# One row of 1024 of most weight chunks goes to GpSimd and ScalarE in the way back of both attentions

## The chip, the cores and the metric

The kernel runs on one core of one Trainium2 chip. The metric is the time of one execution in microseconds (us) of device time, as the median of several executions. The engines are named as in the profile: PE is TensorE, PEld its weight loads, DVE is VectorE, ACT is ScalarE, POOL is GpSimd, and SP is SyncE, which here only issues transfers.

## The reference

A decoding step of four layers for one token, forward and backward: attention, MLP, the same attention again, the same MLP again. Both attentions share `wq`, `wo` and the caches, both MLPs share `w1`, `b1` and `w2`. All data are bf16.

```python
x = x + A(layernorm(x)); x = x + B(layernorm(x))
x = x + A(layernorm(x)); x = x + B(layernorm(x))

# A: D = 1024, 32 query heads, 4 key/value heads, Dh = 128, window W = 4096 of 32768 rows
q = (x @ wq).reshape(32, 128)
p = softmax(q @ k[:, -W:].T * Dh ** -0.5)
return (p @ v[:, -W:]).reshape(4096) @ wo

# B: F = 3584
h = x @ w1 + b1
return (h * tanh(softplus(h))) @ w2
```

The outputs are the step's result and the gradients of all eight arguments for a given gradient of the result: 1024 numbers for `x`, the caches' gradients (two tensors of 4 x 32768 x 128, zero outside the window), and `wq`, `wo`, `w1`, `w2`, `b1`. The core writes 98.6 MB to HBM in all.

## The kernel before

Weights come from HBM in chunks of 1 MB into a ring of eight slots. `Ring.want` lists them in the order of use, and `Ring.pump` (L51, transfer at L68) issues the next load on SP's queue as soon as `Ring.release` has freed a slot. A load therefore waits on SP until the engines that read the old chunk are done with it. The ring's order in the part that matters is `wo` of the second attention (kept from the forward pass), the eight chunks of `wq`, seven of `w2`, eight of `wo`, and five of `wq`; three chunks of `wq` (5, 6 and 7) stay in the ring from one attention's way back to the other's.

The gradient outputs' zero parts are 56 transfers of 1 MB from a tile of zeros. `zeros(n, after)` (L240) issues `n` of them on GpSimd's queue, after a tiny copy on GpSimd that waits for the tile `after`. They are put by hand where they fill the transfer engines.

The way back goes through the second MLP, the second attention (`attn_bwd(1, ...)`), the first MLP, and the first attention (`attn_bwd(0, ...)`). At the end, units of outer products make the weights' gradients, which are evicted into staging tiles and stored from SP's queue (L967, L972).

`attn_bwd` (L822) has two passes over weights. The first multiplies all 4096 rows of `wo` (eight chunks with four rows of 1024 to a partition) with the gradient. The second does it with `wq`, whose chunk `t` has 4096 columns, taken as four pieces of 1024. Between them lie the gradients of the softmax. Each "row" (a 128 x 1024 piece) is done in one of two ways:

- `rowdot` (L401, instruction at L408): one VectorE instruction multiplies the row by the broadcast vector in PSUM (`LB[0]`) and sums it up; the products go to `junk`.
- `turned` (L427): TensorE transposes the row in eight blocks into a PSUM tile (L431), `evac` (L278) copies it back over the row on VectorE (L284) or ScalarE (L287), and later `mv` (L441, instruction at L443) multiplies the eight turned blocks by the vector's columns.

`evac` picks the engine by a running account of charged microseconds, `load`, which `even()` levels. `later` (L415) holds the `mv` calls back until more than `behind[0]` of them wait; a chunk's release stands in the same queue behind its last `mv`. Since everything is issued in this order and each engine works its queue in order, a release is as late as the `mv` ahead of it.

With `DENSE = 2` chunks 0 and 1 of each pass have all four rows turned. From chunk 2 on VectorE does row 0 and the others are turned. In the pass over `wq` of `attn_bwd(0)` the three kept chunks are turned already (`turned_q`).

```python
            behind[0] = max(2, 6 - max(0, c - DENSE + 1))
            rows_chunk(ch, c, GA, l, LB[0], do32, DA, 0 if c < DENSE else 1, None)
            later(lambda c=c: ring.release((*wo_key, c)))
            hooks["do"](c)
```

The hooks put other work between the chunks of the second attention's way back: `conv` turns blocks of the caches, `w1_rest` blocks of `w1`, both with eight transposes and an eviction each.

Of the kernel before, what the change touches and what calls it, by code (L numbers as in the profile page):

```python
# [9 lines left out]
FP32 = mybir.dt.float32  # L10
BF16 = mybir.dt.bfloat16
ACT = mybir.ActivationFunctionType
# [3 lines left out]
P = 128  # L16
# [67 lines left out]
def kernel(  # L84
# [36 lines left out]
    def sb(shape, dtype, name):  # L121
        return keep.tile(shape, dtype, name=name)
# [152 lines left out]
    def even():  # L275
        load["D"] = load["A"] = max(load.values())
# [29 lines left out]
    def bcast(col_of, n, dst=None):  # L306


        for i in range(n):
            k = i % 8  # L310
            nc.tensor.transpose(LB[i // 8][:, k * P:(k + 1) * P], col_of(i).to_broadcast([P, P]), ident_bf[:])  # L311
        if dst is not None:
            nc.vector.tensor_copy(dst, LB[0][:, 0:n * P])
# [84 lines left out]
        return gn  # L398


    def rowdot(w, vecs, n, acc, fours=False):  # L401

        for i, vec in enumerate(vecs):
            out, a = junk[:, 0:n], w[:, i * n:(i + 1) * n]
            if fours:
                out, vec = (x.rearrange("a (k p) -> a k p", p=P) for x in (out, vec))
                a = a.rearrange("a (p k) -> a k p", k=4)
            nc.vector.tensor_tensor_reduce(out=out, in0=a, in1=vec, scale=1.0,  # L408
                                           scalar=acc if i else 0.0, op0=ALU.mult, op1=ALU.add, accum_out=acc)
        load["D"] += len(vecs) * (n * 1.1e-3 + 0.18)  # L410

    lag = deque()
    behind = [2]
# [13 lines left out]
    def turned(w, n, mv, eng=None, block=None):  # L427

        b = big().bitcast(BF16)
        for i in range(n):  # L430
            nc.tensor.transpose(b[:, i * P:(i + 1) * P], block(w, i) if block else w[:, i * P:(i + 1) * P], ident_bf[:])  # L431
        evac(w, b[:, 0:n * P], eng, cost=(0.69 * n / 8, n / 8))
        later(mv, True)
# [7 lines left out]
    def mv(w, n, out, rhs_of, last):  # L441
        for i in range(n):
            nc.tensor.matmul(out, lhsT=w[:, i * P:(i + 1) * P], rhs=rhs_of(i), start=fresh[0], stop=last and i == n - 1,  # L443
                             skip_group_check=True)
            fresh[0] = False

    def rows_chunk(ch, c, col, l, vec, dst, off, nr=2, eng="A"):

        for tt in range(4):
            r = 4 * c + tt  # L450
            if tt < nr:
                rowdot(ch[:, tt, :], [vec], D, dst[:, r:r + 1])
            else:
                w = ch[:, tt, :]
                turned(w, TD, lambda w=w, r=r: mv(w, TD, TP[:, off + r:off + r + 1], lambda i: col[:, i, l:l + 1], True), eng)

    def rows_join(dst, n, off):
        v = dst[:, 0:n].rearrange("p (a b) -> p a b", b=4)[:, :, 2:4]
# [131 lines left out]
    def conv(n, eng=None):  # L590
        for _ in range(n):
            conv_ev(conv_pe(1), eng)
# [224 lines left out]
                rowize_f()  # L817
        return ln_bwd(dnp, sB0["n32"], sB0["rstd"], g, "B0")

    DENSE = 2  # L820

    def attn_bwd(l, sv, g, wo_key, wq_key, wq_keep, hooks, beside=None):  # L822
        name = f"A{l}"
        nc.vector.tensor_copy(GA[:, :, l], g[:])
        bcast(lambda c: GA[:, c, l:l + 1], TD)
        do32 = tmp([P, HQ], FP32, "da")
        mv_open()
        even()
        for c in range(8):
            ch = ring.get((*wo_key, c))  # L830

            behind[0] = max(2, 6 - max(0, c - DENSE + 1))
            rows_chunk(ch, c, GA, l, LB[0], do32, DA, 0 if c < DENSE else 1, None)
            later(lambda c=c: ring.release((*wo_key, c)))
            hooks["do"](c)
        flush()
        for x, n0, k0 in ((0, DENSE, 0), (DENSE, 8, 1)):
            nc.vector.tensor_copy(do32[:, 4 * x:4 * n0].rearrange("p (c k) -> p c k", k=4)[:, :, k0:],
                                  TP[:, DA + 4 * x:DA + 4 * n0].rearrange("p (c k) -> p c k", k=4)[:, :, k0:])
        do_n = from_fours(do32[:])  # L840
        dov = DOC[:].rearrange("p v (g u l h) -> p v g u l h", g=G, u=2, l=2)
        do4 = do_n.rearrange("p (g h) -> p g h", g=G)
        nc.vector.tensor_copy(dov[:, 0, :, 0, l, :], do4)
        nc.gpsimd.tensor_copy(dov[:, 1, :, 1, l, :], dov[:, 0, :, 0, l, :])
        pr = small[:, 64:128]
        prv = pr[:].rearrange("p (g u h) -> p g u h", g=G, u=2)
        o4 = sv["o32"][:].rearrange("p (g h) -> p g h", g=G)
        for u in range(2):
            nc.vector.scalar_tensor_tensor(out=prv[:, :, u, :], in0=do4, scalar=float(D), in1=o4, op0=ALU.mult, op1=ALU.mult)
        sdp = small[:, 224:288]  # L850
        pxv = PX[:].rearrange("p (b l h) -> p b l h", l=2, h=8)
        dsv = DSX[:].rearrange("p (b l h) -> p b l h", l=2, h=8)
        for i in range(2):
            for t in range(16 * i, 16 * i + 16):
                for g_ in range(G):
                    c = scol(g_, t) - 512 * i
                    nc.tensor.matmul(SC[i][:, c:c + 8], lhsT=VS[:, g_, t, :],
                                     rhs=DOC[:, 0, g_ * 32 + l * 8:g_ * 32 + l * 8 + 8], start=True, stop=True)
            if i == 0:
                nc.tensor.matmul(TP[:, 320:384], lhsT=onesD[:], rhs=pr[:], start=True, stop=True)  # L860
                nc.vector.tensor_copy(sdp[:], TP[:, 320:384])
            s = SC[i].rearrange("p (tp c) -> p tp c", c=64)
            nc.vector.tensor_tensor(out=s, in0=s, in1=sdp[:, None, :].to_broadcast([P, 8, 64]), op=ALU.subtract)
# [12 lines left out]
        bcast(lambda c: DQC[:, c, l:l + 1], TD)  # L876
        even()
        hooks["dq"]()
        mv_open()
        bigs.append(SC[1])  # L880
        nc.vector.memset(dnp[:, 0:DENSE], 0.0)
        for t in range(TD):
            key = (*wq_key, t)
            ch = ring.get(key)
            nr = 0 if t < DENSE else 1
            behind[0] = max(2, 6 - max(0, t - DENSE + 1))
            if nr:
                rowdot(ch[:, 0:D], LB[0:1], D, dnp[:, t:t + 1])
            for k in range(nr, 4):
                h0 = 8 * k  # L890
                w = ch[:, h0 * P:(h0 + 8) * P]
                f = lambda w=w, h0=h0, t=t, k=k: mv(w, 8, TP[:, t:t + 1], lambda i: DQC[:, h0 + i, l:l + 1], k == 3)
                if key in turned_q:
                    later(f, True)
                else:
                    turned(w, 8, f)
            if t in wq_keep:
# [22 lines left out]
        zeros(4)  # L920

    def dq3():
        w1_rest(2)
        zeros(3, DQC[:, 0, 1:2])

    def dn3(t):
        if t % 2:
            w1_rest(1)
        if t == 5:
            zeros(1, dnp[:, t:t + 1])  # L930

    g2 = attn_bwd(1, sA1, g3, ("o", 1), ("q", 2), KEEP_Q2,
                  dict(do=lambda c: conv(2), dp=dp3, dq=dq3, dn=dn3))


    W1S = W1[:].rearrange("p t f -> p (t f)")
# [197 lines left out]
        load["D"] += 10  # L1134
        work(4)

    g0 = attn_bwd(0, sA0, g1, ("o", 3), ("q", 3), (), dict(do=do1, dp=dp1, dq=dq1, dn=dn1), units_a0)
# [49 lines left out]
```

## Time and profile before

| | |
|---|---|
| median of 3 runs | 461.53 us (460.98 to 462.93) |
| the profiled execution | 462.39 us, of which 460.62 are its span |
| PE, PEld, DVE, ACT, POOL busy | 337.2, 275.3, 261.3, 228.2, 38.6 us |
| moved by DMA | 183.59 MB, mean 399 GB/s |
| L431 transposes into BIG (PE) | 872, 252 ns each |
| L287 evictions of 128x1024 from BIG to the ring (ACT) | 73, 1013 ns each |
| L284 the same on DVE | 36, 691 ns each |
| L408 rows of 1024 from the ring (DVE) | 38, 1216 ns each |

The span starts with the first instruction; what lies around it is 1.77 us. A slice of the page is a fortieth of the span, 11.5 us. Times of one instruction run from its start to its end, and neighbours on an engine overlap a little, so the pitch of a row of them is shorter: 0.92 us for ACT's eviction of 1.01.

### The profile page before, as it was taken

Reading aid. Unit: us, or ns where it says so; the run is one execution under the profiler, and the core shown is the slowest. Engines: PE = TensorE matmul, PEld = TensorE weight load, DVE = VectorE, ACT = ScalarE, POOL = GpSimd, SP = SyncE. Lnnn points to the kernel's source line nnn. Section 1 sums busy time; section 2 is a strip of 40 time slices with the busy share of each in tenths; the row PEclk is TensorE's granted clock in tenths of the full one; section 3 lists DMA queues with packets and bytes.
Section 4 is the critical chain, followed back from the end, with each engine's and each line's share of the span. In section 5 each row is a group of like instructions: output and inputs, shape, how many; then the busy total and the mean of one; then the engine's idle time right before and its main releaser. Section 6 shows DMA issues by size and latency. Waiting matters only on the chain. (4 is left out here: it accounts for less than half of the span.)

```text
span 460.6 us, 14273 instructions
## 1 busy us (share of the span) xinstructions
PE 337.2 (73%) x6385; PEld 275.3 (60%) x6385; DVE 261.3 (57%) x517; ACT 228.2 (50%) x263; POOL 38.6 (8%) x85
## 2 busy tenths in 40 slices
PE   4836435597678788599879898897896876677950
PEld 3736435497668787599779898787791121112530
DVE  6505731383150149678428786475485987878860
ACT  2502001064035369378128573283267988778850
POOL 4000000000111320100210101102111000000000
PEclk9955555555555569799559855597595555555555
DMA  8999999999999999999999999979999999999995
GB/s 340 420 419 419 419 420 416 422 388 392 393 422 424 418 414 414 406 384 386 376 424 334 407 387 371 414 264 408 424 420 421 419 425 421 427 424 419 408 407 227
DMA packets 28379, 183.59 MB, mean 399 GB/s; under 512 B 3706, under 2 KB 3734, under 8 KB 9494
## 3 DMA queue, kind: packets, MB, share of 16 engines
q1 hardware_dynamic: 20162, 123.94, 67.0%
q0 software_dynamic: 8064, 58.72, 30.7%
q8 instruction: 50, 0.82, 0.7%
q14 instruction: 11, 0.09, 0.0%
q10 hardware_dynamic: 92, 0.02, 0.0%
HBM read 83.94 MB, written 98.62 MB: 396 GB/s over the span
## 5 line engine op out<-in xcount | busy, mean ns | idle before, releaser
L287 ACT COPY ring<-BIG 128x1024 bf16<-128x1024 bf16 x73 | 72.2, 1013 | 40.4 <-PE BIG L431 37.7
L431 PE MATMUL BIG<-ident_bf,ring 128*128 128x128 bf16 x872 | 80.0, 252 | 3.8 <-DMA ring<-in_A_wo_dram 2.0
L431 PEld LDWEIGHTS <-ring 128*128 128x128 bf16 x952 | 69.8, 114 | 5.2 <-DMA ring<-in_A_wo_dram 2.3
L995 PE MATMUL wide<-W 2*128 2x512 bf16 x228 | 48.5, 601 | 19.0 <-DVE ring L284 3.6
L408 DVE CUSTOM_DVE_ANT_0 junk<-ring,SC 128x1024 bf16<-128x1024 bf16 x38 | 46.2, 1216 | 4.5 <-DMA ring<-in_A_wo_dram 1.7
L995 PEld LDWEIGHTS <-W 2*128 2x128 bf16 x240 | 10.9, 103 | 54.5 <-issue 53.8
L443 PEld LDWEIGHTS <-ring 128*128 128x128 bf16 x1024 | 38.2, 100 | 4.6 <-ACT ring L287 4.4
L287 ACT COPY KT<-BIG 128x1024 bf16<-128x1024 bf16 x22 | 21.8, 1015 | 32.3 <-PE BIG L582 30.9
L287 ACT CAST ring<-wide 128x1024 bf16<-128x1024 f32 (+1 forms) x38 | 35.2, 998 | 4.9 <-PE wide L995 4.0
L284 DVE COPY ring<-BIG 128x1024 bf16<-128x1024 bf16 x36 | 24.8, 691 | 20.3 <-PE BIG L431 13.1
L284 DVE CAST ring<-wide 128x1024 bf16<-128x1024 f32 (+1 forms) x26 | 30.2, 1200 | 5.7 <-PE wide L995 5.2
L248 POOL DMA_DIRECT2D out_dram<-zt x56 | 29.6, 534 | 6.3 <-DMA out_dram<-zt 5.6
L553 PE MATMUL MV<-OC,ring 128*128 128x1 bf16 x512 | 16.6, 166 | 15.2 <-DMA ring<-in_A_wo_dram 12.6
L287 ACT COPY W<-BIG 128x1024 bf16<-128x1024 bf16 x20 | 18.9, 1151 | 15.7 <-PE BIG L766 15.7
L553 PEld LDWEIGHTS <-ring 128*128 128x128 bf16 x512 | 16.0, 106 | 16.0 <-DMA ring<-in_A_wo_dram 13.2
L284 DVE CAST VS<-wide 128x1024 bf16<-128x1024 f32 (+1 forms) x18 | 21.0, 1190 | 4.1 <-PE wide L995 3.1
L473 PE MATMUL MV<-NA,ring 128*128 128x1 bf16 x512 | 15.0, 165 | 10.9 <-DMA ring<-in_A_wq_dram 10.0
L601 PE MATMUL MV<-NB,W 128*128 128x1 bf16 x448 | 16.2, 172 | 9.2 <-DMA W<-in_B_w_dram 6.5
L408 DVE CUSTOM_DVE_ANT_0 junk<-ring,DSX 128x1024 bf16<-128x1024 bf16 x18 | 22.0, 1224 | 0.6
L601 PEld LDWEIGHTS <-W 128*128 128x128 bf16 x448 | 15.9, 118 | 9.8 <-DMA W<-in_B_w_dram 7.2
L1046 PE MATMUL wide<-W 32*128 32x256 bf16 x128 | 20.4, 403 | 1.4 <-ACT W L287 0.8
L473 PEld LDWEIGHTS <-ring 128*128 128x128 bf16 x512 | 14.3, 103 | 11.6 <-DMA ring<-in_A_wq_dram 10.6
(256 smaller groups left out, 539.1 us busy)
## 6 DMA issues: line engine op xcount, KB each, us to landing
out_dram<-zt POOLq DMA_DIRECT2D x56, 1024.0 KB, 12.7
ring<-in_A_wq_dram SPq DMA_DIRECT2D x27, 1024.0 KB
ring<-in_A_wo_dram SPq DMA_DIRECT2D x24, 1024.0 KB
ring<-in_B_w_dram SPq DMA_DIRECT2D x14, 1024.0 KB
out_dram<-ring SPq DMA_DIRECT2D x9, 1024.0 KB
W<-in_B_w_dram SPq DMA_DIRECT2D x8, 896.0 KB
ring<-in_A_k_cache_dram SPq DMA_DIRECT2D x4, 1024.0 KB
VS<-in_A_v_cache_dram SPq DMA_DIRECT2D x4, 1024.0 KB
```

What stands on the lines that cost most here:

```text
L248: nc.gpsimd.dma_start(dst, zt[:])
L284: nc.vector.tensor_copy(dst, src)
L287: nc.scalar.copy(dst, src)
L408: nc.vector.tensor_tensor_reduce(out=out, in0=a, in1=vec, scale=1.0, scalar=acc if i else 0.0, op0=ALU.mult, op1=ALU.add, accum_out=acc)
L431: nc.tensor.transpose(b[:, i * P:(i + 1) * P], block(w, i) if block else w[:, i * P:(i + 1) * P], ident_bf[:])
L443: nc.tensor.matmul(out, lhsT=w[:, i * P:(i + 1) * P], rhs=rhs_of(i), start=fresh[0], stop=last and i == n - 1, skip_group_check=True)
L473: nc.tensor.matmul(q_ps[:, h:h + 1], lhsT=ch[:, h * P:(h + 1) * P], rhs=NA[:, t, l:l + 1], start=(t == 0 and h == 0), stop=(t == TD - 1), ...
L553: nc.tensor.matmul(y_ps[:, dd:dd + 1], lhsT=ch[:, tt, dd * P:(dd + 1) * P], rhs=OC[:, h, l:l + 1], start=(h == 0 and dd == 0), stop=(h == ...
L601: nc.tensor.matmul(h_ps[:, fb:fb + 1], lhsT=f_block(W1[:, t], fb), rhs=NB[:, t, l:l + 1], start=(t == 0 and fb == 0), stop=(t == TD - 1), ...
L995: nc.tensor.matmul(b[:, 512 * i:512 * i + 512], lhsT=R[at:at + 2, lo:lo + P], rhs=R[at:at + 2, ro + 512 * i:ro + 512 * i + 512], start=Tru ...
L1046: nc.tensor.matmul(b[:, k * 256:(k + 1) * 256], lhsT=RT[32 * g:32 * g + 32, a, tp, :], rhs=YS[32 * g:32 * g + 32, :], start=True, stop=Tru ...
```

## The change

In both passes of both attentions, row 1 of the first chunks (seven of `wo`, five of `wq`) is no longer turned. A new `pool_dot` gives it to GpSimd, which multiplies its two halves of 512 with a copy of the vector in SBUF, and writes fp32 products into scratch. ScalarE then sums each half with an accumulating copy in place, into `pacc`. These sums are queued in `sums`, and `tick()` issues one after each later turned row of the loop. VectorE adds the two halves at the end of the pass over `wo`, and after chunk 6 of the pass over `wq`.

[...]

In the second attention (`l == 1`) the `DENSE` chunks are none: VectorE does row 0 from chunk 0 on. There the products need `junk` as scratch, so `rowdot` writes its own over the row (`over`), and GpSimd's first half of a `wq` row lands where row 0 was. In the first attention two chunks keep row 0 on TensorE, and the scratch lies in `W1`'s space.

The other work is shifted: four of the `conv` units stand ahead of the pass over `wo` and none at chunks 6 and 7, and six `w1_rest` units stand ahead of the pass over `wq` and none inside it. `behind` counts its steps from chunk 1 as before. The order of transfers on SP's queue is the same.

```diff
+    def pool_dot(w, vec, parts, acc):
+        for i in range(2):
+            n = D // 2
+            a, b, out = w[:, i * n:(i + 1) * n], vec[i], parts[i]
...
+            nc.gpsimd.tensor_tensor(out=out, in0=a, in1=b, op=ALU.mult)
+            def add_up(i=i):
+                nc.scalar.activation(parts[i], parts[i], ACT.Copy, accum_out=acc[i])
+                load["A"] += 0.6
+            sums.append(add_up)
+    def tick():
+        if sums:
+            sums.popleft()()
...
             if tt < nr:
-                rowdot(ch[:, tt, :], [vec], D, dst[:, r:r + 1])
+                rowdot(ch[:, tt, :], [vec], D, dst[:, r:r + 1], over=over)
+            elif tt == 1 and pool is not None:
+                pool(ch[:, tt, :])
             else:
...
+                if tt > 1:
+                    tick()
...
         bcast(lambda c: GA[:, c, l:l + 1], TD)
+        nc.scalar.copy(vec_o, LB[0][:, 0:D])
...
+        hooks["first"]()
         for c in range(8):
...
-            rows_chunk(ch, c, GA, l, LB[0], do32, DA, 0 if c < DENSE else 1, None)
+            if c < np_o:
+                node = lambda w, c=c: pool_dot(w, halves(vec_o), parts_o(None), [pacc[:, i, c:c + 1] for i in range(2)])
+            rows_chunk(ch, c, GA, l, LB[0], do32, DA, 0 if c < DENSE else 1, None, node, l == 1)
...
+        nc.vector.tensor_tensor(out=dov4[:, 0:np_o, 1], in0=pacc[:, 0, 0:np_o], in1=pacc[:, 1, 0:np_o], op=ALU.add)
...
-        bcast(lambda c: DQC[:, c, l:l + 1], TD)
+        bcast(lambda c: DQC[:, c, l:l + 1], 2 * TD)
+        nc.scalar.copy(vec_q, ...)
...
             if nr:
-                rowdot(ch[:, 0:D], LB[0:1], D, dnp[:, t:t + 1])
+                rowdot(ch[:, 0:D], LB[0:1], D, dnp[:, t:t + 1], over=l == 1 and t < np_q)
             for k in range(nr, 4):
+                if k == 1 and t < np_q:
...
+                    pool_dot(ch[:, D:2 * D], v, parts_q(ch), [pacc[:, i, t:t + 1] for i in range(2)])
+                    continue
...
+                if k > 1:
+                    tick()
+            if t == np_q + 1:
+                for i in range(2):
+                    nc.vector.tensor_tensor(out=dnp[:, 0:np_q], in0=dnp[:, 0:np_q], in1=pacc[:, i, 0:np_q], op=ALU.add)
...
     def dq3():
-        w1_rest(2)
+        w1_rest(6)
...
     def dn3(t):
-        if t % 2:
-            w1_rest(1)
...
+    nodes3 = ((DSX[:, 0:1024], lambda ch: [small[:, 0:512], DSX[:, 1024:2048].bitcast(FP32)], 7),
+              (DSX[:].rearrange("p (b l h) -> p b l h", l=2, h=8)[:, :, 0, :],
+               lambda ch: [ch[:, 0:1024].bitcast(FP32), small[:, 0:512]], 5))
     g2 = attn_bwd(1, sA1, g3, ("o", 1), ("q", 2), KEEP_Q2,
-                  dict(do=lambda c: conv(2), dp=dp3, dq=dq3, dn=dn3))
+                  dict(first=lambda: conv(4), do=lambda c: conv(2) if c < 6 else None, dp=dp3, dq=dq3, dn=dn3),
+                  (0, 0), nodes3)
...
+    g0 = attn_bwd(0, sA0, g1, ("o", 3), ("q", 3), (), dict(first=lambda: None, do=do1, dp=dp1, dq=dq1, dn=dn1),
+                  (2, 2), ((NV[0], lambda ch: parts1, 7), (NV[1], lambda ch: parts1, 5)), units_a0)
```

More of the change, by code (lines that the diff above doesn't have):

```diff
@@ L398, in ln_bwd, with rowdot @@
         return gn
-    def rowdot(w, vecs, n, acc, fours=False):
+    def rowdot(w, vecs, n, acc, fours=False, over=False):
         for i, vec in enumerate(vecs):
-            out, a = junk[:, 0:n], w[:, i * n:(i + 1) * n]
+            a = w[:, i * n:(i + 1) * n]
+            out = a if over else junk[:, 0:n]
             if fours:
@@ L410, in rowdot @@
         load["D"] += len(vecs) * (n * 1.1e-3 + 0.18)
+    sums = deque()
+    def pool_dot(w, vec, parts, acc):
+        for i in range(2):
+            n = D // 2
+            a, b, out = w[:, i * n:(i + 1) * n], vec[i], parts[i]
+            if len(b.shape) == 3:
+                a, out = (x.rearrange("p (b h) -> p b h", h=b.shape[2]) for x in (a, out))
+            nc.gpsimd.tensor_tensor(out=out, in0=a, in1=b, op=ALU.mult)
[6 more added lines that the diff above has]
+            sums.popleft()()
     lag = deque()
@@ L445, in mv, with rows_chunk @@
             fresh[0] = False
-    def rows_chunk(ch, c, col, l, vec, dst, off, nr=2, eng="A"):
+    def rows_chunk(ch, c, col, l, vec, dst, off, nr=2, eng="A", pool=None, over=False):
         for tt in range(4):
@@ L818, in dn_b0, with halves, attn_bwd @@
         return ln_bwd(dnp, sB0["n32"], sB0["rstd"], g, "B0")
-    DENSE = 2
-    def attn_bwd(l, sv, g, wo_key, wq_key, wq_keep, hooks, beside=None):
+    pacc = sb([P, 2, TD], FP32, "pacc")
+    def halves(ap):
+        return [ap[:, 0:512], ap[:, 512:1024]]
+    def attn_bwd(l, sv, g, wo_key, wq_key, wq_keep, hooks, dense, nodes, beside=None):
         name = f"A{l}"
+        DENSE, DENSE_Q = dense
+        (vec_o, parts_o, np_o), (vec_q, parts_q, np_q) = nodes
         nc.vector.tensor_copy(GA[:, :, l], g[:])
         bcast(lambda c: GA[:, c, l:l + 1], TD)
+        nc.scalar.copy(vec_o, LB[0][:, 0:D])
         do32 = tmp([P, HQ], FP32, "da")
@@ L828, in attn_bwd @@
         even()
+        hooks["first"]()
         for c in range(8):
             ch = ring.get((*wo_key, c))
-            behind[0] = max(2, 6 - max(0, c - DENSE + 1))
-            rows_chunk(ch, c, GA, l, LB[0], do32, DA, 0 if c < DENSE else 1, None)
+            behind[0] = max(2, 6 - max(0, c - 1))
+            node = None
+            if c < np_o:
+                node = lambda w, c=c: pool_dot(w, halves(vec_o), parts_o(None), [pacc[:, i, c:c + 1] for i in range(2)])
+            rows_chunk(ch, c, GA, l, LB[0], do32, DA, 0 if c < DENSE else 1, None, node, l == 1)
             later(lambda c=c: ring.release((*wo_key, c)))
@@ L836, in attn_bwd @@
         flush()
-        for x, n0, k0 in ((0, DENSE, 0), (DENSE, 8, 1)):
-            nc.vector.tensor_copy(do32[:, 4 * x:4 * n0].rearrange("p (c k) -> p c k", k=4)[:, :, k0:],
-                                  TP[:, DA + 4 * x:DA + 4 * n0].rearrange("p (c k) -> p c k", k=4)[:, :, k0:])
+        while sums:
+            tick()
+        dov4 = do32[:].rearrange("p (c k) -> p c k", k=4)
+        tp4 = TP[:, DA:DA + HQ].rearrange("p (c k) -> p c k", k=4)
+        if DENSE:
+            nc.vector.tensor_copy(dov4[:, 0:DENSE, 0:1], tp4[:, 0:DENSE, 0:1])
+        nc.vector.tensor_tensor(out=dov4[:, 0:np_o, 1], in0=pacc[:, 0, 0:np_o], in1=pacc[:, 1, 0:np_o], op=ALU.add)
+        nc.vector.tensor_copy(dov4[:, np_o:, 1], tp4[:, np_o:, 1])
+        nc.vector.tensor_copy(dov4[:, :, 2:], tp4[:, :, 2:])
         do_n = from_fours(do32[:])
@@ L875, in attn_bwd @@
         nc.vector.tensor_scalar(out=DQC[:, :, l], in0=dq_ps, scalar1=scale, scalar2=None, op0=ALU.mult)
-        bcast(lambda c: DQC[:, c, l:l + 1], TD)
+        bcast(lambda c: DQC[:, c, l:l + 1], 2 * TD)
+        nc.scalar.copy(vec_q, LB[1][:, 0:D].rearrange("p (b h) -> p b h", h=8) if len(vec_q.shape) == 3 else LB[1][:, 0:D])
         even()
@@ L880, in attn_bwd @@
         bigs.append(SC[1])
-        nc.vector.memset(dnp[:, 0:DENSE], 0.0)
+        if DENSE_Q:
+            nc.vector.memset(dnp[:, 0:DENSE_Q], 0.0)
         for t in range(TD):
@@ L884, in attn_bwd @@
             ch = ring.get(key)
-            nr = 0 if t < DENSE else 1
-            behind[0] = max(2, 6 - max(0, t - DENSE + 1))
+            nr = 0 if t < DENSE_Q else 1
+            behind[0] = max(2, 6 - max(0, t - 1))
             if nr:
-                rowdot(ch[:, 0:D], LB[0:1], D, dnp[:, t:t + 1])
+                rowdot(ch[:, 0:D], LB[0:1], D, dnp[:, t:t + 1], over=l == 1 and t < np_q)
             for k in range(nr, 4):
                 h0 = 8 * k
+                if k == 1 and t < np_q:
+                    v = vec_q
+                    v = [v[:, 0:64], v[:, 64:128]] if len(v.shape) == 3 else halves(v)
+                    pool_dot(ch[:, D:2 * D], v, parts_q(ch), [pacc[:, i, t:t + 1] for i in range(2)])
+                    continue
                 w = ch[:, h0 * P:(h0 + 8) * P]
@@ L896, in attn_bwd @@
                     turned(w, 8, f)
+                if k > 1:
+                    tick()
+            if t == np_q + 1:
+                assert not sums
+                for i in range(2):
+                    nc.vector.tensor_tensor(out=dnp[:, 0:np_q], in0=dnp[:, 0:np_q], in1=pacc[:, i, 0:np_q], op=ALU.add)
             if t in wq_keep:
@@ L1135, in units_a0 @@
         work(4)
-    g0 = attn_bwd(0, sA0, g1, ("o", 3), ("q", 3), (), dict(do=do1, dp=dp1, dq=dq1, dn=dn1), units_a0)
+    NV = [RT[:, a, 8 * i:8 * i + 8, :].rearrange("p t s -> p (t s)") for a in range(2) for i in range(2)]
+    parts1 = [x.bitcast(FP32) for x in NV[2:]]
+    g0 = attn_bwd(0, sA0, g1, ("o", 3), ("q", 3), (), dict(first=lambda: None, do=do1, dp=dp1, dq=dq1, dn=dn1),
+                  (2, 2), ((NV[0], lambda ch: parts1, 7), (NV[1], lambda ch: parts1, 5)), units_a0)
     g0b = sb([P, TD], BF16, "g0b")
```

## The prediction

> **What bounds the kernel now.** I read the page's slices first, then two-microsecond windows of the way back, then the waits of SP's queue, then the timelines of the engines. Names: *do1* and *dn1* are the `wo` and `wq` passes of `attn_bwd(1)` (192.3-220.1 and 231.7-258.1 us), *do0* and *dn0* those of `attn_bwd(0)` (292.9-317.7 and 329.2-346.6 us).
>
> ```profile
> DMA  8999999999999999999999999979999999999995
> GB/s 340 420 419 419 419 420 416 422 388 392 393 422 424 418 414 414 406 384 386 376 424 334 407 387 371 414 264 408 424 420 421 419 425 421 427 424 419 408 407 227
> ```
>
> The transfers bound the whole: 183.59 MB at the 420 GB/s of an undisturbed slice are 437 us of the 460.6. After 345 us every slice but the last moves 407-426 GB/s, the last eviction (L284, 444.05 + 1.22 us) is over 15 us before the end, and the zeros and stores are a fixed number of bytes. So the chain view, which follows only the last 130 us through compute, misleads here: only time in which the queues run empty or thin can be won, and that lies between 192 and 316 us.
>
> ```profile
> 244.00:246.00 2.00, 2.00 (x57) 2.00 (x54) 1.95 (x5) 1.79 (x2) 0.00 (x0) 1.00 0.72 168
> 246.00:248.00 2.00, 2.00 (x55) 2.00 (x53) 1.62 (x4) 1.93 (x2) 0.00 (x0) 1.00 0.86 336
> 300.00:302.00 2.00, 2.00 (x57) 2.00 (x55) 1.67 (x3) 1.76 (x3) 0.00 (x0) 1.00 0.12 47
> 302.00:304.00 2.00, 2.00 (x56) 2.00 (x55) 1.69 (x4) 1.79 (x3) 0.00 (x0) 1.00 0.76 197
> ```
>
> Columns: PE, PEld, DVE, ACT, POOL, clock, DMA share, GB/s. Two holes, both with PE full. Their cause is in SP's waits: a ring slot is loaded again only when TensorE has finished the chunk in it.
>
> ```profile
> SPq L68 <- PE TP L443: 67.3, 33, 5.3
> ```
>
> ```profile
> 202.05 18.44 SPq L68 DMA_DIRECT2D ring<-in_A_wq_dram  x8
> 244.28 25.42 SPq L68 DMA_DIRECT2D ring<-in_B_w_dram  x7
> 301.38 4.45 SPq L68 DMA_DIRECT2D ring<-in_A_wo_dram  x3
> ```
>
> The holes stand right before the first reload of dn1 (244.28) and of do0 (301.38): the zeros issued before them have run out. Against 420 GB/s the windows lose 3.1 us in 192-226, 2.7 in 244-256, 2.2 in 268-290 and 4.8 in 298-316, some 13 us: the most this change could win. Since the queue is empty at 300 us, what happened to transfers earlier no longer counts there. **The end moves as the first reload of do0 (301.38) moves**, plus what the thin stretch behind it gains.
>
> **The costs of one item**, from these rows (durations) and their pitch back to back:
>
> ```profile
> 300.98 1.21 DVE L408 CUSTOM_DVE_ANT_0 junk<-ring,SC 128x1024 bf16<-128x1024 bf16 x1
> 301.01 1.93 ACT L287 COPY ring<-BIG 128x1024 bf16<-128x1024 bf16 x2 [0.24 <-PE BIG L431]
> 302.51 0.69 DVE L284 COPY ring<-BIG 128x1024 bf16<-128x1024 bf16 x1 [0.31 <-PE BIG L431]
> 301.21 0.61 PE L431 MATMUL BIG<-ident_bf,ring 128*128 128x128 bf16 x8
> 301.66 0.34 PE L443 MATMUL TP<-GA,ring 128*128 128x1 bf16 x8
> ```
>
> A row on VectorE: 1.27 us (with its 0.08 accumulator read). A row over TensorE: 0.45 + 0.20 us of PE at full clock (0.85 + 0.20 at half), and an eviction of 0.92 on ACT or 0.65 on DVE. New are two operations. A *product* is GpSimd's 512-element multiply. Nothing in the trace multiplies there; nearest are
>
> ```profile
> 1.01 0.29 POOL masks.py:199 TENSOR_SCALAR_AFFINE_SELECT ident_bf<-ident_bf 128x128 bf16<-128x128 bf16 x1
> 1.75 3.56 POOL L173 MEMSET zt<- 128x4096 bf16 x1
> ```
>
> 512 elements are 0.45 us at the memset's rate (no input) and 1.16 at four selects (one input). A product reads two tensors, so I take **1.1**, near the select, and carry up to 1.65 (half as much again for the second input). A *sum* is ScalarE's 512 fp32 values with an accumulator: three 128x512 casts at 348.75 us take 0.49 each; I take **0.6** (accumulator read included; DVE's takes 0.08) and carry 0.49 to 0.92, ACT's price of 1024. A row moved to GpSimd so takes 0.65 us from PE and one eviction from ACT or DVE, and gives ACT 1.2 us: for ACT and DVE together it is no saving. It helps only where PE is the bound.
>
> [...]
>
> **do1, worked along the queues.** Before, PE carried 26 rows and 14 conversions of 0.45 us: 16.9 + 6.3 = 23.2 us, plus what half clock (to 196.2) and the broadcast add: 192.3 to 220.1. After: 17 rows, 17.4 us. Now ACT is the bound: copy of the vector 1.0, 14 evictions 12.9, 14 sums 8.4 = 22.3 us from 193.4, so 215.7, some waits at the start, last products at 217.1; DVE has 8 rows and 17 evictions, 21.2 us. Minus 3.0 us, plus one more small operation (0.2): **-2.8**. GpSimd needs 2.2 us a chunk where ACT and DVE need 2.7: hidden, and POOL has no zeros queued in this pass. With sums at 0.85 ACT has 3.5 us more. The first reload is later: a chunk now has two products to queue instead of four, so `behind` frees chunk 0 only in chunk 3, behind 17 evictions where 13 stood, with sums between them; I get 205.3 for 202.05. The four zeros end at 204, so a new hole of some 3 us opens here; the reloads then come bunched (205, 206, 208, ...) and the last of them two us earlier. This hole is paid back by the hole at 244, which closes.
>
> **dn1.** The broadcast is 8 transposes longer (0.85 at half clock) and four `w1_rest` units are moved ahead of the pass: about 3.4 us at half clock, less what the earlier full clock gives; chunk 0 starts at 238.7 for 236.9. After that PE has 19 rows, 12.4 us, in place of 26 rows and 4 units. But GpSimd's first output lands in the chunk's row 0, so it waits for VectorE's row 0, which stands behind four `w1` evictions: first product at 240.8. Five pairs at 2.2 are 11, to 251.8; a last sum 0.6; behind it in ACT's queue stand six evictions, 5.5; last products 0.5: 258.4 for 258.1. **+0.3**; I add 0.6 for clock, below: **+0.9**. Each 0.1 us on a product is 1 us here. Queued behind the waiting sums on ACT are evictions, and behind those PE's buffers; on POOL one zero. Chunk 0 is free some 0.4 us earlier counted from the pass's start.
>
> **w2 and `dn_b0`** (260-292): unchanged; 14 VectorE rows of 1.27 hold them. They shift.
>
> **do0.** Chunk 0 is released after 8 queued rows in place of 9: the walk gives 300.5 for 301.4, chunks 1 and 2 302.0 and 302.9 for 303.57 and 305.51 (**-0.9**). The three `wo` loads they start then run close together, and the thin stretch to 314 gains some **0.5** of its 2 us. GpSimd's pair of chunk 2 is done at 302, in time.
>
> **dn0**: GpSimd ends around 344.4 with two zeros issued in between, its last sum and VectorE's last row at 346.3: no change against 346.6, and zeros cover the queues to 362.
>
> Sum: -2.8 + 0.9 - 0.9 - 0.5 = **-3.3 us**. The profiled execution took 462.39 (span 460.62 + 1.77), which would become 459.1; it lies 0.86 above the median, so the median 461.53 becomes **458.2**.
>
> **Rivals.**
> *GpSimd sets the pace (slower).* At 2.0 us a product dn1 ends at 240.8 + 20 + 6.6 = 267.4 (+9.3), do1 at some 223.5 (+3.4), first reload of do0 unchanged: about +12, 474. The point from which it decides: dn1 costs 10 us for each us that a product takes over 1.07, do1 14 us for each over 1.35 (a pair then exceeds its 2.7 us a chunk), and the other terms give 3.6; so 1.4 us is even and 1.5 is 0.5% slower, 464. For it: two inputs; against it: the select's 1.16 holds four fixed costs. Chance 0.20.
> *Dear sums.* At 0.85 do1 is 0.7 longer instead of 2.8 shorter and dn1 2.3 longer than forecast, ACT's 0.92 + 1.7 a chunk then exceeding GpSimd's pair: +2.5, 464. Against it: the casts' 0.49. Chance 0.08.
> *The new hole costs.* If the queue is not empty before do0, the 3 us at 204 are not paid back by the closed holes and the gain is about 1: 460.5. For it: both come from the same bytes. Chance 0.11.
> *PE loses its clock.* In 312-316, where PE transposes some 40% of the time, the granted clock falls to 0.5; in 308-312, at some 53%, it holds. dn1's two rows in 2.2 us are 40%. [...] At 1.05 us a row PE keeps GpSimd's pace but not the last chunks: +0.6, which I booked; with half clock through do1 too another 1.5, 459.7. Chance 0.06.
>
> **Numbers.** My forecast has 0.55. A measurement of this kernel tells about 0.5%, 2.3 us, from no change, so 459.2 to 463.8 is the same. The forecast's own spread (products 0.9 to 1.2, sums 0.5 to 0.65) is 455 to 460, of which 0.48 is faster and 0.07 the same. GpSimd's pace gives 0.18 to slower and 0.02 to the same, dear sums half of their 0.08 to each, the new hole and the clock all their 0.17 to the same: faster 0.48, same 0.30, slower 0.22. The range goes from 455.0, the forecast's cheap end, to 465.0, where a product takes some 1.53 us; beyond that lies most of GpSimd's rival, and little else.
>
> **What would show it.** Right: the first `wq` reload at 205, a thin window at 204-207; do1's end at 217; no hole at 244 and under 1 us of one before do0; products at 1.1 and sums at 0.6. Wrong: products over 1.45 with ACT waiting for POOL through dn1; a clock of 0.5 in do1; the stretch from do0's first reload to the end longer than 159 us.

## The result, and the profile after

The changed kernel took 466.68 us (median of 4 runs, 464.65 to 467.58) beside 461.25 us for the kernel before (460.91 to 462.93): a ratio of 1.0104, 95% interval 1.0062 to 1.0146. It is slower by 5.4 us, where 3.3 us of gain were forecast. Its profiled execution took 467.58 us with a span of 465.72, 5.1 longer than the span before. Each time is the median of the runs in the fast state; one run of experiment 7, at 474.20 us, was in the slow one.

The slices of the page after (DMA busy in tenths, GB/s moved; a slice is now 11.6 us):

```profile
DMA  8999999999999999989999999879997999999997
GB/s 336 423 418 420 418 419 417 421 398 354 400 421 423 420 420 417 416 335 422 398 423 386 384 375 348 325 257 409 422 425 291 410 412 419 417 420 418 404 407 316
```

The weak slice around 244 us (334 before) has 386 now: that hole closed, as forecast. But the slice around 309 us, thin already, fell to 257 of 264, the one before it to 325 of 414, and slice 31, around 355 us, from 421 to 291. Windows show these places close up, with columns as in the prediction. The kernel before:

```profile
306.00:308.00 2.00, 1.85 (x51) 1.73 (x49) 1.69 (x4) 1.74 (x3) 0.00 (x0) 1.00 0.91 340
350.00:352.00 2.00, 1.24 (x9) 0.32 (x9) 0.00 (x0) 1.30 (x5) 0.00 (x0) 0.50 0.99 414
352.00:354.00 2.00, 1.16 (x9) 0.18 (x6) 1.54 (x2) 2.00 (x3) 0.00 (x0) 0.50 1.03 430
```

The kernel after:

```profile
300.00:302.00 2.00, 2.00 (x61) 2.00 (x59) 2.00 (x4) 0.00 (x0) 0.02 (x1) 1.00 0.17 68
302.00:304.00 2.00, 0.11 (x5) 0.04 (x2) 1.47 (x3) 0.72 (x2) 2.00 (x2) 1.00 0.56 197
306.00:308.00 2.00, 2.00 (x34) 2.00 (x34) 1.06 (x2) 2.00 (x5) 1.87 (x3) 0.53 0.04 8
```

```profile
350.00:352.00 2.00, 2.00 (x39) 1.80 (x37) 0.14 (x1) 2.00 (x6) 1.87 (x3) 0.50 0.25 102
352.00:354.00 2.00, 0.35 (x14) 0.26 (x10) 1.97 (x4) 1.85 (x5) 1.98 (x5) 0.50 0.27 94
```

In 300-302 ScalarE and GpSimd do nothing (0.00 and 0.02 of 2 us), and right behind that TensorE does nothing (0.11). The queues are nearly dry at 300 to 304, as they were before (47 and 197 GB/s); new are the hole at 306 and the one at 350 to 354. What stopped GpSimd stands in its timeline (start, duration, group, and in brackets the idle time ahead of it with what ended it):

```profile
301.98 11.50 POOL L424 TENSOR_TENSOR W<-ring,W 128x512 f32<-128x512 bf16 x10 [4.03 <-DMA W<-W]
...
343.36 9.09 POOL L424 TENSOR_TENSOR W<-ring,W 128x512 f32<-128x512 bf16 x8 [9.11 <-DMA W<-W]
352.39 0.17 POOL L243 COPY pz<-dnp 1x1 f32<-1x1 f32 x1
352.51 1.12 POOL L248 DMA_DIRECT2D out_dram<-zt  x2
```

Two waits for a transfer, `W<-W`: 4.03 us in do0 ahead of chunk 1's product, and 9.11 us in dn0 ahead of chunk 0's. SP's timeline shows which transfers these are, and what they did to the reloads:

```profile
298.88 1.37 SPq L1021 DMA_DIRECT2D W<-W  x2
301.34 7.56 SPq L68 DMA_DIRECT2D ring<-in_A_wo_dram  x3
310.28 10.98 SPq L68 DMA_DIRECT2D ring<-in_A_wq_dram  x5
335.02 1.74 SPq L1021 DMA_DIRECT2D W<-W  x2
```

L1021 is `rowize`, which lays a gradient out as rows for the outer products at the end: that of `GA` at 298.88, that of `DQC` at 335.02. Both write columns of `W1`'s tile below 5120 and read columns below 6656. The change put the first attention's vector and products into the same tile, in `RT`, columns 6656 to 10752. No byte is shared, but the built program has GpSimd's product wait for these transfers. The waits pass down the queues. ScalarE's next instruction is the sum of that product:

```profile
303.17 0.63 ACT L427 ACTIVATE W<-W 128x512 f32<-128x512 f32 x1 [4.32 <-POOL W L424]
```

Behind the sum stand evictions, behind those TensorE's buffers (it sits idle for 3.83 us, to 305.94, until an eviction of ScalarE's has ended), and behind TensorE the release of chunk 1: the three reloads come at 301.3, 307.1 and 308.4, for 301.4, 303.6 and 305.5 before. In dn0 the wait also holds back the zeros: those for `t == 3` stand on GpSimd's queue behind eight products and are issued at 352.5. The queues have run dry by 350.

The bytes moved say what the two waits cost. Against 420 GB/s the queues lose 4.5 us in 304-318 for 1.6 before, and 3.6 in 344-366 for nothing before; behind 430 us, where they run out of work, they lose 2.1 less (3.7 for 5.8). That makes 4.4 of the 5.1 us by which the span grew.

### The profile page after: what moved, and what is told of

It is laid out like the page before. It is cut to its first block, busy times and chain, and to the rows that moved or that the text cites. A ratio compares the mean times of both kernels' runs of the same rounds, so it can differ in the third digit from the quotient of the medians.

```text
span 465.7 us, 13569 instructions
## 1 busy us (share of the span) xinstructions
PE 329.2 (71%) x5953; PEld 266.0 (57%) x5953; DVE 263.4 (57%) x528; ACT 238.6 (51%) x338; POOL 92.8 (20%) x133
## 5 line engine op out<-in xcount | busy, mean ns | idle before, releaser
L454 PE MATMUL BIG<-ident_bf,ring 128*128 128x128 bf16 x672 | 69.0, 271 | 18.4 <-ACT ring L287 16.0
L454 PEld LDWEIGHTS <-ring 128*128 128x128 bf16 x728 | 59.8, 123 | 19.9 <-issue 18.1
L287 ACT COPY ring<-BIG 128x1024 bf16<-128x1024 bf16 x54 | 53.9, 1006 | 21.7 <-PE BIG L454 20.6
L410 DVE CUSTOM_DVE_ANT_0 junk<-ring,SC 128x1024 bf16<-128x1024 bf16 x29 | 35.3, 1216 | 6.4 <-ACT junk L427 2.7
L466 PEld LDWEIGHTS <-ring 128*128 128x128 bf16 x800 | 32.0, 105 | 9.9 <-ACT ring L287 9.3
L284 DVE COPY ring<-BIG 128x1024 bf16<-128x1024 bf16 x30 | 20.4, 689 | 25.3 <-PE BIG L454 19.9
L424 POOL TENSOR_TENSOR W<-ring,W 128x512 f32<-128x512 bf16 x24 | 27.0, 1151 | 14.9 <-DMA W<-W 13.1
L581 PEld LDWEIGHTS <-ring 128*128 128x128 bf16 x512 | 16.0, 106 | 14.3 <-DMA ring<-in_A_wo_dram 13.0
L427 ACT ACTIVATE W<-W 128x512 f32<-128x512 f32 x24 | 15.1, 629 | 15.0 <-POOL W L424 14.9
L287 ACT COPY W<-BIG 128x1024 bf16<-128x1024 bf16 x19 | 17.9, 1169 | 9.0 <-PE BIG L794 9.0
```

The source lines that it names most:

```text
L284: nc.vector.tensor_copy(dst, src)
L287: nc.scalar.copy(dst, src)
L424: nc.gpsimd.tensor_tensor(out=out, in0=a, in1=b, op=ALU.mult)
L427: nc.scalar.activation(parts[i], parts[i], ACT.Copy, accum_out=acc[i])
L581: nc.tensor.matmul(y_ps[:, dd:dd + 1], lhsT=ch[:, tt, dd * P:(dd + 1) * P], rhs=OC[:, h, l:l + 1], start=(h == 0 and dd == 0), stop=(h == ...
```

## The experiments

Two measures are used beside the time: the first reload of do0, and the stretch from it to the end of the span. That stretch is 159.2 us before and 164.4 after, so the loss that shows lies behind 301 us. The first reload comes at the same time in both (301.38 and 301.34). A profile is one execution, though, and executions differ in unchanged code as well: the fourteen profiles reach do1 at 187.7 to 191.9 us, the kernel before at 191.9 and the kernel after at 190.0.

The theories. *W*: the loss comes from the scratch's place, through the two waits for row stores. *C*: it comes from TensorE's clock, which dn1 lost as the fourth rival feared. *P*: products and sums cost time wherever they stand. Each time below is compared with runs of the kernel before on the same chip (medians 460.95 to 461.29 us). The changed kernel has four runs that spread over 2.9 us, so a difference from its median is good to some 1.5 us, by an estimate from that spread.

**1. Only the second attention.**

```diff
-                  (2, 2), ((NV[0], lambda ch: parts1, 7), (NV[1], lambda ch: parts1, 5)), units_a0)
+                  (2, 2), ((NV[0], lambda ch: parts1, 0), (NV[1], lambda ch: parts1, 0)), units_a0)
```

> attn_bwd(1) as in the changed kernel, attn_bwd(0) as before. Theory W (the loss lies in the first attention, where GpSimd waits for row stores into another part of the W1 tile): the second attention's part is nearly neutral, 461 to 462.5 us, with the first reload of do0 at 301 to 303 and no window under 200 GB/s in 346-360. Theory C (the loss comes from TensorE's half clock in dn1 and its longer pass): 464 to 466. Theory P (each product and sum costs wherever it stands): half of the loss, 464.

461.98 us, ratio 1.0004 (0.9977 to 1.0030). First reload of do0 at 301.2, stretch 159.4 us. The second attention's part is neutral, which speaks for W and against C and P. It is also no gain.

**2. Only the first attention.**

```diff
-                  (0, 0), nodes3)
+                  (2, 2), nodes3)      # nodes3 with 0 and 0 rows, conv and w1_rest placed as before
```

> attn_bwd(0) as in the changed kernel, attn_bwd(1) as before. Theory W: all of the loss is here, 465 to 467 us, GpSimd's product of do0's chunk 1 waiting some 4 us and that of dn0's chunk 0 some 9 us for W1's own transfers, and the queues nearly dry for some 4 us around 350. Theory C: dn1 is as before, so 460 to 462. Theory P: 464.

464.83 us, ratio 1.0068 (1.0044 to 1.0091). GpSimd waits 12.0 us for `W<-W`, the second and third reload of do0 come 6.8 and 8.1 us behind the first, and the stretch is 163.6 us. The loss is here, though not all of it: 3.5 us of 5.4, with the second attention nearly free by itself. The two parts do not quite add up. By this time alone P, which expects 464, is as near as W; experiments 1 and 3 part the two.

**3. The first attention's scratch out of the `W1` tile.**

```diff
-            a, b, out = w[:, i * n:(i + 1) * n], vec[i], parts[i]
+            a, b = w[:, i * n:(i + 1) * n], vec[i]
+            out = parts[i] if parts else a          # in place, bf16
...
-                  (2, 2), ((NV[0], lambda ch: parts1, 7), (NV[1], lambda ch: parts1, 5)), units_a0)
+                  (2, 2), ((junk[:], lambda ch: None, 7), (junk[:], lambda ch: None, 5)), units_a0)
```

> The changed kernel with attn_bwd(0)'s vector in the free scratch row (VectorE writes its products over the weight row that it has read) and GpSimd's products written in place over their weight row in bf16: nothing of the first attention's products stands in the W1 tile. Theory W: the waits of 4 and 9 us are gone, dn0 ends 8 us earlier, the queues do not run dry around 350: 461 to 462.5 us, 4 to 5 less than the changed kernel. Theories C and P: products and sums are as many as before, so 465.5 to 467.

460.05 us, ratio 0.9964 (0.9938 to 0.9989): 6.6 us less than the changed kernel, more than W expected. The same places of its windows and of SP's timeline:

```profile
300.00:302.00 2.00, 1.68 (x48) 1.61 (x45) 2.00 (x4) 2.00 (x5) 2.00 (x3) 1.00 0.72 184
302.00:304.00 2.00, 0.78 (x16) 0.69 (x15) 1.92 (x4) 2.00 (x6) 2.00 (x3) 1.00 1.16 410
...
350.00:352.00 2.00, 1.89 (x11) 0.46 (x8) 1.93 (x3) 2.00 (x4) 0.00 (x0) 0.50 1.01 423
```

```profile
299.37 2.71 SPq L68 DMA_DIRECT2D ring<-in_A_wo_dram  x3
```

ScalarE and GpSimd are busy throughout 300-302, the three reloads come within 2.7 us instead of 7.6, and 350-352 moves 423 GB/s instead of 102. As many products and sums are made as in the changed kernel, so P falls. In dn1 the granted clock is 0.50 in 244-252 in both kernels, so the 6.6 us are not C's either.

**4. TensorE kept busy in dn1.**

```diff
+    def spin(n):
+        for i in range(n):
+            nc.tensor.transpose(idle[:].bitcast(BF16)[:, i * P:(i + 1) * P], ident_bf[:], ident_bf[:])
...
+                if l == 1:
+                    spin(4)
                 if key in turned_q:
```

> The changed kernel with four extra TensorE transposes of the identity ahead of each row that TensorE turns in dn1 (into a PSUM bank that nothing reads), so that TensorE stays busy between GpSimd's pairs. Theory C: the granted clock stays at 1.0 from 241 us on, dn1 takes 29 us for 31.0, and the end comes 2 us earlier or more: 462 to 464.5. Theory W: the clock comes back but the end stays within 1 us, 465.5 to 467, as the first reload of do0 is covered by the later waits.

469.42 us, ratio 1.0156 (1.0120 to 1.0192): slower than the changed kernel. Windows of dn1, first of the changed kernel, then of this one:

```profile
236.00:240.00 4.00, 1.85 (x34) 1.73 (x31) 4.00 (x8) 2.26 (x4) 2.43 (x3) 1.00 0.99 416
...
244.00:248.00 4.00, 3.60 (x56) 3.31 (x55) 1.77 (x3) 4.00 (x10) 4.00 (x5) 0.50 1.00 373
```

```profile
244.00:248.00 4.00, 3.04 (x70) 2.75 (x67) 3.14 (x6) 3.77 (x9) 4.00 (x5) 1.00 1.01 399
```

The clock did come back (1.00 for 0.50), but dn1 takes 30.8 us for 31.0, where C expects 29. From the first product to the last sum's read both take 12.1 us (237.57 to 249.66 and 239.54 to 251.63), since GpSimd's ten products, 1.11 us apart, set that time; from there to dn1's end this kernel takes 9.8 us for 10.3, with the extra transposes in it. C falls by its own expectation and by experiment 3. But the kernel is slower than W expects too (465.5 to 467), and where its 2.7 us go is not shown: its profiled execution loses 1.0 us in do1 and 0.9 in `dn_b0`, neither of which the edit touches.

**5 and 6. One pass of the first attention mended at a time.** In 5 only do0 has the edit of experiment 3, in 6 only dn0.

> Of attn_bwd(0)'s two passes only do0 has its vector and products out of the W1 tile; dn0 keeps them there. By the windows the changed kernel loses 3.4 us more than the kernel with both mended in 304-318 (the late reloads of do0) and 3.5 us more in 346-360 (dry queues behind dn0's wait). If the two add up: 463.3 us, reloads of do0 within 1 us of each other from 300 on, and dn0's first product still waiting some 9 us. If dn0's wait alone matters: 466; if do0's alone: 460.

461.70 us, ratio 1.0003 (0.9986 to 1.0021). Reloads at 299.1, 300.8 and 301.7; the wait in dn0 is still there (8.86 us).

> The mirror: only dn0 mended, do0 with its scratch in the W1 tile. If the two add up: 463.2 us, the second reload of do0 still some 5 us behind the first, no thin window in 346-360. If dn0's wait alone matters: 460; if do0's alone: 466.

464.81 us, ratio 1.0090 (1.0065 to 1.0114). The wait in do0 stays (3.90 us; reloads at 299.8, 305.4 and 306.7), and in 348-354 all windows move 422 GB/s or more.

By the medians do0's wait is worth 5.0 us taken away alone (466.68 to 461.70) and 4.8 taken away last (464.81 to 460.05), dn0's 1.9 and 1.7, and both together 6.6. So they nearly add up, but not in the shares that the two expectations rested on (3.4 and 3.5 us by the windows): both missed by 1.6 us. The shares are uncertain. The interval of experiment 6 overlaps that of the changed kernel, and the stretches behind the first reload (164.4 us in the changed kernel, 161.2 in 5, 161.7 in 6, 158.5 in 3) give 3.2 and 2.7. Why the 9 us wait costs no more than the 4 us one can be read from the windows: in do0 the queues are empty already (68 GB/s in 300-302), in dn0 four zeros issued at 332 cover part of it (422 GB/s in 333-345), and the end gives some of the rest back. Behind 430 us the queues lose 3.5 to 3.7 us in the kernels with dn0's wait (the changed one, 2 and 5) and 5.5 to 5.8 in those without it (before, 3 and 6).

**7. The row stores moved behind the products.** The scratch stays in `W1`.

```diff
-        if c == 0:
+        if c == 7:
             rowize(GA, TD, 32, 0)
...
-        rowize(DQC, HQ, 0, NOFF)
         zeros(4, DQC[:, 0, 0:1])
...
-        if t == 4:
-            twins()
         if t == 5:
+            rowize(DQC, HQ, 0, NOFF)
+            twins()
```

> The changed kernel with scratch, products and sums where they are (fp32, in the W1 tile), but the row stores that GpSimd waits for moved behind the last product of each pass: those of GA from chunk 0 to chunk 7 of do0, those of DQC and the twins to chunk 5 of dn0. Theory W (it is the order of these transfers and not the form of the products): 460 to 462 us, no wait of POOL for a transfer of W1, reloads of do0 within 1 us of each other, no thin window in 346-360. Rival F (the in-place bf16 form is cheaper by itself, and that is what gained): 465 to 467. In between if the twins' later start costs at the end.

467.16 us, ratio 1.0139 (1.0108 to 1.0169): as slow as the changed kernel, far from W's number and next to F's. F has no cost to show, though: a product takes 1.15 us and a sum of 512 takes 0.63 in both forms (last section). GpSimd's two waits did go (one of 2.15 us, for an earlier pair of `W<-W` transfers, stands ahead of do0's first product), and the reloads came at 299.4, 302.0 and 302.9. But who else reads the rows now waits for them. The tile `W`'s instructions sat idle for `W<-W` 13.1 us in 2 waits in the changed kernel; here, by cause (us, times),

```profile
  DMA W<-W: 23.3, 7
```

and TensorE's outer products wait as well:

```profile
354.76 0.60 PE L1059 MATMUL BIG<-W 2*128 2x512 bf16 x2 [6.83 <-DMA W<-W]
```

The units that make the stores start later (their first product into `wide` at 358.7 us, 347.5 in experiment 3), and 358-360 moves 48 GB/s. The rows are wanted early, so it is the scratch that has to give way, not the transfers. This run removes W's waits without a gain in time; that W explains the loss rests on experiments 2, 3, 5 and 6.

**8. One sum a row, all products in place.** In both attentions the products stand in their row, and one sum of 1024 takes the place of two of 512.

```diff
-            def add_up(i=i):
-                nc.scalar.activation(parts[i], parts[i], ACT.Copy, accum_out=acc[i])
-                load["A"] += 0.6
-            sums.append(add_up)
+        def add_up():
+            nc.scalar.activation(w, w, ACT.Copy, accum_out=acc[0])
+            load["A"] += 1.1
+        sums.append(add_up)
```

> All products in place in bf16 in both attentions, and ScalarE adds up a row in one instruction of 1024 instead of two of 512. Theory S (the term of my sum that was short is the sum's price, 0.63 + 0.19 us instead of 0.6, and ScalarE holds do1 and dn1): a row costs ScalarE 0.92 + 0.19 = 1.1 us instead of 1.64, do1 is 1 to 3 us shorter and dn1 2 us: 457 to 459 us. Rival (GpSimd's two products of 1.15 us hold the pair, and the hole at 204 takes what do1 gains): 459.5 to 460.5, as with both mended.

458.98 us, ratio 0.9948 (0.9929 to 0.9966). dn1 takes 27.1 us. Which of the two edits did that, experiment 10 tells.

**9. Experiment 8 without the second attention.**

> The kernel with one sum a row (458.98 us), but attn_bwd(1) as before: only the first attention has GpSimd's rows. If the second attention's part carries its share now that its sums are cheap (its dn1 took 27.1 us there for 28.4 before, and do0's first reload came at 298.5 for 301.4): 461 us, 2 more than with both. If what happens before the queues run empty at 300 does not count and do0 alone gains: 459.

460.17 us, ratio 0.9989 (0.9963 to 1.0015). The interval, 459.5 to 461.9 us, holds the first expectation and no change, and not the second: the second attention carries a share, some 1.2 us by the medians. The first reload of do0 does not show it: it comes at 298.4 here and at 298.5 in experiment 8, since the pass over `w2` ends at 280.7 us in both (more on this at 12).

**10. All products in place, two sums a row.**

```diff
-    nodes3 = ((DSX[:, 0:1024], lambda ch: [small[:, 0:512], DSX[:, 1024:2048].bitcast(FP32)], 7),
+    nodes3 = ((DSX[:, 0:1024], lambda ch: None, 7),
               (DSX[:].rearrange("p (b l h) -> p b l h", l=2, h=8)[:, :, 0, :],
-               lambda ch: [ch[:, 0:1024].bitcast(FP32), small[:, 0:512]], 5))
+               lambda ch: None, 5))
```

> All products in place as in the kernel with one sum a row, but two sums of 512 a row again. It parts that kernel's 1.1 us over the kernel with only the first attention's products in place. If the sums' price is what counts there (0.55 us of ScalarE a row): 460 us, dn1 29.5 us. If it was the scratch of the second attention (the 3 us that its first product waits for the transfer out of DSX, and the waits for the one scratch row): 459, dn1 27 to 28 us.

457.70 us, ratio 0.9926 (0.9904 to 0.9948): below both expected times, with dn1 (27.5 us) where the second expects it. The sum's price is not what counted: with two sums it is no slower than with one. The second attention's scratch counted too, by the medians (460.05 in experiment 3, where it stays; the two intervals overlap by a little). Dn1's first product, in the changed kernel and in this one:

```profile
237.57 1.15 POOL L424 TENSOR_TENSOR ring<-ring,DSX 128x512 f32<-128x512 bf16 x1 [6.86 <-ACT ring L287]
```

```profile
230.09 11.19 POOL L425 TENSOR_TENSOR ring<-ring,DSX 128x512 bf16<-128x512 bf16 x10 [1.24 <-ACT DSX L924]
```

In the changed kernel it writes over row 0 and so has to wait until VectorE has done that row, at 237.4 (the line names ScalarE's eviction, which had ended at 237.1). It starts 8.7 us after `DQC`, here 3.1, and dn1 takes 27.5 us for 31.0. In do1 the 3.09 us wait for the transfer out of `DSX` and those for the one scratch row are gone as well, and do1 takes 27.3 us for 28.4.

**11 and 12. A chunk released sooner.** 11 is experiment 8 and 12 is experiment 10, each with

```diff
-            behind[0] = max(2, 6 - max(0, c - 1))
+            behind[0] = max(2, 4 - max(0, c - 1))
```

and the same in the pass over `wq`.

> The kernel with one sum a row, with four queued rows instead of six behind which a chunk's products are held back at a pass's start, so that the chunk is released a chunk earlier. A chunk has two rows for TensorE where it had four, so six rows are three chunks. If the hole at 204 and the one before do0 come from that: first wq reload 202 for 204.3, first reload of do0 297 for 298.5, 457 to 458 us. If TensorE then waits for evictions instead: 459 or more.

457.57 us, ratio 0.9922 (0.9899 to 0.9945); first `wq` reload at 201.0, first reload of do0 at 297.3.

> All products in place, two sums of 512 a row, and four queued rows instead of six at a pass's start. The two edits act at different places (products no longer wait for scratch; chunks are released a chunk earlier). If they add up: 456 to 457 us, first wq reload 200 to 201.5, first reload of do0 296.5. If the second is worth nothing by itself, as the run with one sum left open: 457.7.

457.59 us, ratio 0.9921 (0.9894 to 0.9949); first `wq` reload at 201.6, first reload of do0 at 297.0. In 11 the expectation came true. In 12 the reloads moved about as expected and the time did not: 457.6 as experiment 10. Three kernels (10, 11, 12) agree at 457.6, below both the kernel before and the changed one.

Most of what dn1 wins is lost again in the pass over `w2` behind it. In experiments 8 to 12 dn1 ends between 250.7 and 256.0 us, yet the pass over `w2` ends at 280.1 to 280.7 in all five. TensorE waits there for the loads of `w2` (`ring<-in_B_w_dram`), 1.3 to 5.3 us in all, which it does not in the kernel before, and when the pass ends 114.0 MB have been moved in each of the five. That agrees with the prediction's first reading, that the transfers bound the whole, though the queues are not quite full there (384 to 403 GB/s).

## Why the prediction was wrong, point by point

**The step that failed** is the first attention's, twice. "GpSimd's pair of chunk 2 is done at 302, in time" and "GpSimd ends around 344.4 ... no change" took a product to start as soon as its chunk and GpSimd were there. GpSimd began the pair of chunk 1 only at 301.98 and ended that of chunk 2 at 306.5; in dn0 it ended at 355.9. The working named what GpSimd's first output waits for in dn1, but not what its output in `W1`'s space waits for. The prices hidden there are, by the medians, some 5.0 us in do0 and 1.9 in dn0, for terms of 0. The diff named the place (`NV`, in `RT`); `W<-W` transfers stand in the profile before, as many as after; what it took was to ask which transfers touch that tile while the products run. None of the rivals was this one, so the time fell outside the range.

**"The end moves as the first reload of do0 moves"** held before and in the mended kernels: the stretch is 159.2 us before, 158.5 in experiment 3, 158.1 in 10, 158.9 in 8. After, it is 164.4, which the prediction had written down as a sign of its being wrong (over 159).

**The prices.** A product was put at 1.1; here are the product and the sum from the profile after:

```profile
L424 POOL TENSOR_TENSOR W<-ring,W x24: 1138/1151/1167, 295.7 to 354.8; 128x512 f32<-128x512 bf16 x24
L427 ACT ACTIVATE W<-W x24: 618/630/634, 297.3 to 356.0; 128x512 f32<-128x512 f32 x24
L427 ACT ACTIVATION_READ_ACCUMULATOR W<-W x24: 185/187/193, 297.8 to 356.5; 128x1 f32 x24
```

1.15 us, at a pitch of 1.11 (two halves take 2.26 to 2.27). The largest rival, GpSimd's pace, did not come. The sum was put at 0.6: two of them with their reads take 1.33 us of ScalarE (305.79 to the eviction at 307.12), 0.67 each, short of the dear sums of 0.85.

**The spread.** The sizes of do1 and dn1 below are from single executions. The code of the changed kernel's do1 took 28.2 to 30.5 us in seven profiles (after, 1, 3 to 7) and 29.5 to 30.7 in the three without the second attention's part (before, 2, 9); dn1 took 29.1 to 31.0 in six (after, 1, 3, 5 to 7) and 28.1 to 29.3 in those three. So a difference of 1 us between two profiles says little.

**do1** (from the gradient that it starts with to GpSimd's copy of `DOC`) went from 29.5 to 28.4 us: 1.1 instead of 2.8 gained. The working left out the wait of 3.09 us for the transfer out of `DSX` and 2.2 us for the one scratch row; without these do1 gains 2.2 (experiment 10). The first `wq` reload came at 204.4 for 205.3 forecast, with the thin window behind it; counted from do1's start that is 14.3 us for 13.4, as this execution started do1 earlier.

**dn1** (`DQC` to its gradient) went from 28.4 to 31.0: +2.7 for +0.9. Counted from `DQC` the first product came after 8.7 us (9.1 forecast) and the last sum's read ended after 20.8 (20.7). What was too short is the end: 8.1 us from there to the last products (249.66 to 257.80), where 6.0 were put down and 0.6 for the clock. TensorE does its last seven rows there, most of them 1.1 us apart at half clock. With products in place dn1 takes 27.5, so the term's sign came from the scratch, not from the work.

**The first reload of do0** was to be 2.8 us earlier by the sum, 0.9 of them in do0 itself, and came at 301.3, as before. do0's own part nearly came true: 8.3 us from its gradient to the reload, for 8.9 before. From do1's start to do0's the changed kernel took 2.5 us longer, where 1.9 less were forecast; 1.9 of that are hidden, as its execution had reached do1 that much sooner. The two reloads behind it, forecast at 302.0 and 302.9, show the wait: 307.1 and 308.4.

**The clock's rival** happened as a reading: 0.50 in dn1 from 241.3 to 254.9. It may have cost more than the 0.6 us booked. The same code of dn1 took 29.1, 29.9 and 29.2 us where half clock came back for 6.8 us (1, 5, 7) and 31.0, 29.7 and 30.8 where it came back for 13.7 (after, 3, 6), some 1 us more on average. The reading behind this rival was rough, too: over 312-316 of the kernel before transposes fill 2.30 of 4 us, not 40% (that holds for 312-314), against 2.21 in 308-312. (Of the bounds that the prediction starts from, 192-226 loses 3.5 us and not 3.1; nothing else rests on it.)

**The hole at 244** closed (414 and 397 GB/s in 242-246 for 406 and 168).

With all scratch out of the way the change gains 3.5 us (experiment 10), near the 3.3 forecast. That is luck in good part. By its profile do1 gives 2.2 us for 2.8, dn1 0.8 for a loss of 0.9, do0's way to the first reload 1.0 for 0.9 and the stretch behind it 1.1 for 0.5; but the pass over `w2`, which was to shift unchanged, takes 25.6 us for 23.1.

## What to carry to other kernels

Where an engine's output or scratch is put can decide when it may start. For each new instruction list what else touches the tile that it writes, transfers above all, and when those land; here a shared tile cost waits of 4.03 and 9.11 us though no byte is shared. An engine in the middle of a chain can pass such a wait on: behind GpSimd's 4.03 us ScalarE sat idle for 4.32 and TensorE for 3.83, and this wait of an engine that is idle four fifths of the time (20% busy in the kernel after) cost about as much of the whole (5.0 us by the medians, 3.2 by the profiles). And a transfer that others need could not be moved out of the way here (experiment 7); the scratch can, here at no cost, since a weight row that has been read is scratch.

## What the runs showed of the hardware

GpSimd's multiply of 512 elements took the same 1.15 us whether it wrote fp32 into another tile or bf16 over its own input (1151 ns in the kernel after, 1150 in experiment 10), and with a strided vector as second input (1153 in the dn1 of the kernel after). ScalarE's sum took 0.63 us for fp32 (the kernel after) and for bf16 (experiment 10) alike, and 1.06 for 1024 elements (experiment 8).

A small row store could be slow to land here. In the kernel after `GA`'s (2 KB each), issued at 298.88 with thin queues (216 GB/s in 298-302), let GpSimd go at 301.98, 3.1 us later; `DQC`'s (8 KB each), issued at 335.02 with full ones (422 GB/s in 333-345), at 343.36, 8.3 us later, while nearly all the traffic was zeros. The share of the queues' packets in 333-345:

```profile
q0 software_dynamic: 656, 4.78, 95.1%
q1 hardware_dynamic: 145, 0.25, 5.4%
```

The second case took 2.7 times as long as the first, with stores four times as large and 4.78 MB of zeros beside them; which of the two counts, no run shows.

TensorE's clock after one and the same gap went two ways. In dn1 of the kernel after and of experiment 1, in this order:

```profile
240.42 0.61 PE L454 MATMUL BIG<-ident_bf,ring 128*128 128x128 bf16 x8 [2.57 <-ACT ring L287]
```

```profile
240.91 0.61 PE L454 MATMUL BIG<-ident_bf,ring 128*128 128x128 bf16 x8 [2.57 <-ACT ring L287]
```

Both wait 2.57 us. The first falls to half clock at 241.3, the second only at 246.9, after two more gaps of 1.23 and 0.77 us. Between 192 and 262 us the granted clock changes at 193.5, 217.4, 234.4, 241.3, 254.9 and 258.3 in the first run and at 195.6, 219.6, 233.2, 246.9, 253.7 and 260.5 in the second (by the clock of its windows): within each run these times lie multiples of 3.41 us apart, to 0.1 us. Divided by them into stretches of 3.41, the gap lies whole in one stretch of the first run (237.9 to 241.3), and is cut at 240.0 in the second, 1.7 us on one side and 0.9 on the other. That the two runs differ for this reason is the author's estimate. The clock fell behind a stretch with 2.57 us idle in the first run; in the second a stretch with 1.69 us idle kept it and one with 1.75 lost it. How much idleness it takes, the two runs do not settle: in the first a stretch with 1.37 us idle (196.9 to 200.3) kept it, and one with 1.05 (254.9 to 258.3) lost it.
